# Attention with projected keys, then a gated layer: the first block's output as seven products, and three kinds of preparation moved into or out of the list-scheduled part

## The chip, the cores and the metric

The kernel runs on one core of a Trainium2 chip. The time is that of the device in microseconds, from the start of the program to its end; 517.52 us is the median of three runs of the kernel before (517.07 to 517.91). A profile is one execution taken by the hardware profiler; its span is 515.9 us.

A core has engines that each work through their own queue of instructions in order: TensorE (PE, matmuls, and PEld for loading their weights), VectorE (DVE), ScalarE (ACT), GpSimd (POOL) and SyncE (SP, which here only starts transfers). They wait for each other through semaphores. Matmuls write to eight banks of PSUM, called pF0 to pF3 and pA0 to pA3 in the kernel, each 128 partitions by 512 float32 values.

## The reference

```python
# attention: q, k, v are (8, 8, 1024, 64); E, F are (64, 1024)
k_proj = np.einsum('ks,bhsd->bhkd', E, k)
v_proj = np.einsum('ks,bhsd->bhkd', F, v)
scores = (1 / np.sqrt(64)) * np.matmul(q, k_proj.transpose(0, 1, 3, 2))
attn = softmax(scores)                  # over the 64 projected keys
attn_out = np.matmul(attn, v_proj)
# x is attn_out as (8192 tokens, 512)
# gated layer: w_gate, w_val are (512, 1536), w_out is (1536, 512)
gate = 1 / (1 + np.exp(-(x @ w_gate)))
out  = (gate * (x @ w_val)) @ w_out
```

## The kernel before

The 8192 tokens are 16 blocks of 512, two to a batch. The hidden layer of a block, `gate * val`, is kept as `hT` (1536 features on twelve tiles, 512 tokens). The output of a block is the product of that with `w_out` (`wO`).

Nearly every product of the gated layer is done as two-by-two blocks with seven products instead of eight (Winograd's form of Strassen's method). For the output the factors are sums of quarters of `hT` (`S1`, `S2`, and two made in place) and of `wO` (`T1` to `T4`). The sums are made by VectorE:

```python
def t_sums(n):        # 128 x 1536 each
    o, a, b, op, r, w = {
        3: (T3, B22, B12, ALU.subtract, ...), 2: (T2, T3, B11, ALU.add, ...),
        4: (T4, B21, T2, ALU.subtract, ...),  1: (B12, B12, B11, ALU.subtract, ...),
    }[n]
    dve(lambda e: e.tensor_tensor(o, a, b, op), r, w, t=0.95)

def s_sums(blk, n, ms, eng="DVE"):   # ms: which of six tile rows
    o, a, b, op, r, w = {
        1: (S1, A21, A22, ALU.add, "A21 A22", "S1"),
        2: (S2, S1, A11, ALU.subtract, "S1 A11", "S2"),
        3: (A21, A11, A21, ALU.subtract, "A11 A21", "A21"),
        4: (A12, A12, S2, ALU.subtract, "A12 S2", "A12"),
    }[n]
    ...
```

`product` is one of the seven: 12 matmuls of 128x256. Partial results that two quarters of the output share are copied out of a bank and into another one in between: `seed` copies bank a to bank c with ScalarE, `keep_snap` copies a bank to a half of `EF`, and `add_snap` adds a bank and such a half with VectorE.

The program has two parts. In the first, instructions stand in the order in which the code issues them: blocks 0 and 1 of the hidden layer, and the attention of batches 0 and 1. Block 0 is computed by plain products (`mstep`), and its output too:

```python
def oproj(blk, tt, pb, cols=((0, DM),)):       # 128 tokens, 12 matmuls of 128x512
    for m in range(NF):
        mm(pb, bank[pb][:, 0 : c1 - c0], hT[blk % 2][:, m, tt * P : (tt + 1) * P],
           wO[:, m, c0:c1], ..., start=(m == 0), stop=(m == NF - 1))
    dve(lambda e: e.tensor_scalar(o[:, c0:c1], bank[pb][...], 0.5, None, op0=ALU.mult), ...)
    FF.append(pb)
    add("SP", lambda e: e.dma_start(out_v[...], o[:, c0:c1]), ...)
```

The value half of block 1 is done as a chain of seven products on two banks a and c, in three steps (K = 3, 4, 5). `FF` is the list of free F banks:

```python
def p1():
    held_v["a"], held_v["c"] = a, c = FF.two()
    v_product(blk, q, a, "A11", "B11", start=True)
    seed(a, c)
def p26():
    v_product(blk, q, c, "A12", "B21", stop=True)
    v_product(blk, q, a, "S2", "T2")
    v_snap(0, a)
    hidden(K, 0, 0, bank[c][:, :], [], b=c)
# ... p57, p4
def p3():
    v_product(blk, q, c, "S4", "B22", stop=True)
    v_add(0, c)                       # VectorE, frees bank c
    FF.append(c)
    hidden(K, 1, 0, vsnap[0][:, :], [("vsnap", 0)])
```

The attention of batch 1 lies between these, in pieces that take banks from two lists, `FF` and `AA`:

```python
def mixed3():
    f, a0, a1 = FF.two(), AA.two(), AA.two()
    sc_one(3, f)                      # scores of head pair 3
    xo_one(0, a0); xo_one(1, a1)      # attention outputs of pairs 0 and 1
    for g in range(2):
        exp_half(3, g, f); FF.append(f[g])
    later("A0", x_half, 0, a0, AA)    # ScalarE copies to xu, which free the banks
    later("A1", x_half, 1, a1, AA)
def outputs3():
    f, a0 = FF.two(), AA.two()
    bd = AA.take()
    den8(bd)                          # sums of the exponentials
    xo_one(2, f); xo_one(3, a0)
    ...                               # copies to xu, reciprocals, split
def bc(rnd):                          # broadcast the reciprocals, then four multiplies into xT
    bks = [AA.take() for _ in range(4)]
    ...
```

In the code's order, `todo` is a list of slots and `put` and `on` hang further pieces after a slot:

```python
for m in range(2, NF):
    todo.append(lambda m=m: mstep(0, m))
# ...
on(3, 0, h_sums(1, Z, 1, 2, 3))
for tt in range(4):
    todo.append(lambda tt=tt: oproj(0, tt, FF.take()))
on(3, 1, n1["outputs"])
on(3, 2, lambda: n1["bc"](0))
on(3, 3, lambda: n1["bc"](1))
```

The second part is recorded as tasks with a goal and an assumed length, and a list scheduler (`arranged`) puts them in order on each engine. It covers the output of block 1, the other 14 blocks and the attention of the batches from 2 on:

```python
for n in (3, 2):
    t_sums(n)
for n in (3, 2, 4):
    gt_sums(n)                        # weight sums of w_gate, 128 x 1536
gt_sums(1)
for n in (1, 2, 3, 4):
    xs_sums(2, n)
next_kv(2, -2.0)                      # projection of keys and values of batch 2
transpose_q(["kpB"])
t_sums(4)
t_sums(1)
o_chain(1, OA, OC, 0.0, 2.0, sums=False)
```

Of the kernel before, what the change touches and what calls it, by code (L numbers as in the profile page):

```python
# [237 lines left out]
def bass_linformer_attn__then__ffn_glu_sigmoid_kernel(  # L238
# [18 lines left out]
    with contextlib.ExitStack() as es:  # L257
# [30 lines left out]
        identf = within([P, P], FP32)  # L288
        bsel8f = within([P, 4, 2, 64], FP32)
        early[0], used[0] = wT[:, :, :, :].rearrange("p a b c -> p (a b c)"), 0  # L290
        bsel8 = within([P, 4, 2, 64], BF16)
        kp = within([P, NR, DH], BF16)
        rhi = within([P, 256], BF16)
        rhl = within([P, 256], BF16)
        early[0], used[0] = gT[:, :, :, :].rearrange("p a b c -> p (a b c)"), 0
        rden = within([P, 256], FP32)
        rows = within([P, 4, 32], FP32)
        ident = within([P, P], BF16)
# [173 lines left out]
        def start_loads():  # L472
            for src, rows, n in ((E, slice(0, 64), "E"), (F, slice(64, 128), "F")):
                add(
                    "SP",
                    lambda e, src=src, rows=rows: e.dma_start(EF[rows, :], src[:, :]),
                    w=[("EF", n)],
                    dma="in" + n,
                )
            for i in range(4):  # L480
                pool(
                    lambda e, i=i: e.memset(quad[32 * i : 32 * i + 32, :], 32.0 * i),  # L482
                    w=[("quad", i)],
                )
            for R in range(2):
                load_kv_heads(0, k, R)
                load_q_half(0, 0, R)
            for R in range(2):
                load_kv_heads(1, v, R)
            load_w(0, 0)  # L490
            load_w(0, 1)
            load_w(1)
            load_w(2)
            for R in range(2):
                load_q_half(0, 1, R)
            load_w(3)
            load_w(4)
            load_w(5)

        def heads8():  # L500
# [454 lines left out]
        def attention(b):  # L955
# [87 lines left out]
                    [("rhl", R) for R in range(2)],  # L1043
                )

            def bc(rnd):
                bks = [AA.take() for _ in range(4)]
                for half_ in range(2):
                    for j in range(4):
                        jj = slice(32 * j, 32 * j + 32)  # L1050
                        mm(
                            bks[j],
                            bank[bks[j]][:, 256 * half_ : 256 * half_ + 256],
                            bsel8[jj, 2 * half_ + rnd, :, :].rearrange("p h d -> p (h d)"),
                            rhl[jj, 0:256],
                            ["bsel8", ("rhl", j // 2)],
                            tp=(32 * j, 0),
                        )
                for j in range(4):
                    n = 4 * rnd + j  # L1060
                    mul(n // 2, n % 2, bks[j])
                    AA.append(bks[j])

            def xo_one(r, bks):
                for g in range(2):
# [216 lines left out]
        def mm_one(blk, m, i, n, pb):  # L1282
# [8 lines left out]
                stop=(i == NI - 1),  # L1291
            )

        def gate(blk, m, pg, pv):
            M = blk * NF + m
# [17 lines left out]

        def oproj(blk, tt, pb, cols=((0, DM),)):
            o = vsnap[tt][:, :] if tt < 2 else ost[:, tt, :]
            ok = [("vsnap", tt)] if tt < 2 else None
            t = 2 * (2 * (blk % 2) + tt % 2) + tt // 2
            for n, (c0, c1) in enumerate(cols):
                if n:
                    pb = FF.take()  # L1320
                for m in range(NF):
                    mm(
                        pb,
                        bank[pb][:, 0 : c1 - c0],
                        hT[blk % 2][:, m, tt * P : (tt + 1) * P],
                        wO[:, m, c0:c1],
                        [("hT", blk % 2, m, tt // 2)] + (["wO0", "wO12"] if m < H6 else ["wO1"]),
                        start=(m == 0),
                        stop=(m == NF - 1),
                    )  # L1330
                dve(
                    lambda e, pb=pb, c0=c0, c1=c1: e.tensor_scalar(
                        o[:, c0:c1], bank[pb][:, 0 : c1 - c0], 0.5, None, op0=ALU.mult
                    ),
                    [],
                    ok or [("ost", tt, x) for x in ((0, 1) if len(cols) == 1 else (n,))],
                    b=pb,
                )
                FF.append(pb)
                add(  # L1340
                    "SP",
                    lambda e, c0=c0, c1=c1: e.dma_start(out_v[blk // 2, t][:, c0:c1], o[:, c0:c1]),
                    r=ok or [("ost", tt, x) for x in ((0, 1) if len(cols) == 1 else (n,))],
                    dma=f"out{tt}" if n == 0 else "outlast",
                )

        H6 = NF // 2

        def t_sums(n):
            B11, B12 = wO[:, 0:H6, 0:256], wO[:, 0:H6, 256:512]
            B21, B22 = wO[:, H6:NF, 0:256], wO[:, H6:NF, 256:512]
            T4, T3, T2 = [wT[:, i, :, :] for i in range(3)]
            o, a, b, op, r, w = {
                3: (T3, B22, B12, ALU.subtract, ["wO1", "wO12"], [("wT", 3)]),
                2: (T2, T3, B11, ALU.add, ["wO0", ("wT", 3)], [("wT", 2)]),
                4: (T4, B21, T2, ALU.subtract, ["wO1", ("wT", 2)], [("wT", 4)]),  # L1360
                1: (B12, B12, B11, ALU.subtract, ["wO0"], ["wO12", ("wT", 1)]),
            }[n]
            if n == 4:
                w = w + ["bsel8", ("kp", 0), ("kp", 1)]
                w += [(k, R) for k in ("rhi", "rhl") for R in range(2)]
            dve(lambda e: e.tensor_tensor(o, a, b, op), r, w, t=0.95)

        def s_sums(blk, n, ms, eng="DVE"):
# [4 lines left out]
            S1, S2 = hS[:, 0, lo, :], hS[:, 1, lo, :]  # L1373
# [13 lines left out]

        def part(blk, x, up):
            if x[0] == "S":
                return [(x, m) for m in up]  # L1390
            return [("hT", blk % 2, m + H6 * (x[2] == "2"), int(x[1]) - 1) for m in up]

        def product(blk, bk, A, B, start=False, stop=False, js=(0, 1), ms=(0, NF // 2), also=()):
            h = hT[blk % 2]
            for j in js:
                for m in range(*ms):
                    if A[0] == "S":
                        lhsT = hS[:, int(A[1]) - 1, m, j * P : (j + 1) * P]
# [64 lines left out]
        def evac(bk, tok, col):  # L1463
            o, keys = quarter(tok, col)
            act(o, bank[bk][:, :].rearrange("p (j c) -> p j c", j=2), [], keys, b=bk, scale=0.5)

        def o_chain(blk, a, c, goal, step, sums=True):
            turn = [0]
# [123 lines left out]
        def gt_sums(n, part=None):  # L1592
# [15 lines left out]
            if n != 1:  # L1608
                w += ["rows", "ident"] + [("rden", c, R) for c in range(2) for R in range(2)]
# [327 lines left out]

        A, Z = (0, 4), (4, 6)
        todo.append(lambda: first_pair(0, lambda: xo(1)))
        for m in range(2, NF):  # L1940
            todo.append(lambda m=m: mstep(0, m))
        qt2, sc2, den2, bc2, xo2 = half_unit(1, att)
        put(3, lambda: (qt2(0, ("DVE", "ACT")), qt2(1, ("DVE", "ACT"))))
        put(4, lambda: (sc2(0), sc2(1)))
        put(4, second_loads)
        put(6, lambda: (den2(), xo2(0), xo2(1)))
        put(7, lambda: (vt_sums(3, 0), vt_sums(2, 0)))
        put(8, lambda: bc2(0)())
        put(9, lambda: bc2(1)())
        put(10, x_sums(1, 1, 2))  # L1950
# [51 lines left out]
                on(u, 0, lambda: [late1(x, g) for x in ("A0", "A1") for g in range(2)])  # L2002
        on(2, 0, h_sums(1, A, 1))
        on(2, 4, h_sums(1, A, 2, 3))
        on(3, 0, h_sums(1, Z, 1, 2, 3))
        for tt in range(4):
            todo.append(lambda tt=tt: oproj(0, tt, FF.take()))
        on(3, 1, n1["outputs"])
        on(3, 2, lambda: n1["bc"](0))
        on(3, 3, lambda: n1["bc"](1))  # L2010

        for i, slot in enumerate(todo):
            slot()
# [9 lines left out]
        def when(K):  # L2023
            return PACE * (K - 6)

        blocks_ready(1)
        blocks_ready(2)

# [4 lines left out]
            vd_one(XA, 0, b % 2)  # L2033
            vd_one(XA, 1, b % 2, b > 3)

        for n in (3, 2):
            t_sums(n)
        for n in (3, 2, 4):
            gt_sums(n)
        gt_sums(1)  # L2040
        for n in (1, 2, 3, 4):
            xs_sums(2, n)
        next_kv(2, -2.0)
        transpose_q(["kpB"])
        t_sums(4)
        t_sums(1)
        o_chain(1, OA, OC, 0.0, 2.0, sums=False)
        for n in (1, 2, 3, 4):
            xs_sums(3, n)
# [78 lines left out]
```

The softmax here doesn't subtract the row's maximum and nothing guards it: scores larger than these inputs give would overflow.

## Time and profile before

| | |
|---|---|
| time, median of 3 (us) | 517.52 |
| span of the profile (us) | 515.9 |
| VectorE busy in 60-70, 70-80, 80-90 us (of 10 each) | 8.0, 8.8, 9.5 |
| ScalarE busy in the same (of 10 each) | 8.0, 5.5, 4.4 |
| one 128x512 VectorE operation from PSUM (us) | 0.69 |
| one 128x512 ScalarE copy from PSUM (us) | 0.60 |
| sum of weights, 128x1536 bf16, VectorE (us) | 0.95 |

The profile names an instruction by the line of the helper that recorded it, so all matmuls have line 385, and one tells them apart by the tensors they read and the bank they write. The start of one matmul to the start of the next is what it costs; its own busy time (0.27 us for 256 columns) overlaps the following ones. VectorE's and ScalarE's operations too start about 0.1 us before the one ahead has ended by the profile.

### The profile page before, as it was taken

How to read it: one execution, taken by the hardware profiler on the slowest of the kernel's cores; microseconds unless marked ns; L12 is line 12 of the kernel's file. 1: busy time of each engine (PE TensorE's matmuls, PEld its weight loads, DVE VectorE, ACT ScalarE, POOL GpSimd, SP SyncE). 2: the span in 40 equal slices, each digit the busy share in tenths (PEclk: the TensorE clock that was granted, in tenths of full speed). 3: DMA queues.
4: the chain of work that ended last, by engine and by line, in shares of the span. 5: the costliest groups of instructions: out<-in, count | busy, mean ns of one | idle time of the engine just before them, and what ended most of it. 6: DMA issues, size and time to landing. Idle time of an engine off the chain costs nothing.

```text
span 515.9 us, 11369 instructions
## 1 busy us (share of the span) xinstructions
PE 505.0 (98%) x4598; PEld 410.0 (79%) x4598; DVE 410.9 (80%) x809; ACT 345.0 (67%) x645; POOL 41.0 (8%) x60
## 2 busy tenths in 40 slices
PE   5999999999999999999999999999999999999996
PEld 3545645888888888888888888888888888888885
DVE  4548779899789796988879888797969898777774
ACT  2555683867778677677767776777676766676652
POOL 9420301200200020000100020000000000000000
PEclk9999999999999999999999999999999999999999
DMA  9999999899798788454946389374104330201013
GB/s 161 199 198 204 150 195 221 115 178 233 93 224 155 152 150 138 102 125 123 174 85 154 60 152 203 56 164 100 46 7 97 42 104 1 83 1 76 6 43 124
DMA packets 105205, 63.13 MB, mean 122 GB/s; under 512 B 63040, under 2 KB 97344, under 8 KB 105152
## 3 DMA queue, kind: packets, MB, share of 16 engines
q0 software_dynamic: 34000, 29.89, 37.5%
q1 hardware_dynamic: 71152, 32.52, 28.8%
q8 instruction: 36, 0.59, 0.4%
q14 instruction: 17, 0.14, 0.1%
HBM read 60.29 MB, written 16.78 MB: 149 GB/s over the span
## 4 chain that ended last, share of the span: by engine, by line
PE 94%; DMA 2%; DVE 1%; POOL 1%; issue 0%; ACT 0%; DVEq 0%; POOLq 0%
PE pA L385 51%; PE pF L385 43%; DMA KVs<-in_v_dram 2%; DVE hT L1832 0%; POOL KVs L403 0%; DVE vsnap L1710 0%; POOL Qb L403 0%; DVE xT L868 0%; DVE ost L1437 0%; ACT sig L389 0%; DVE sig L1786 0%; ACT vsnap L389 0%; DVE ost L1522 0%; POOL quad L482 0%; DVE hS L1382 0%
## 5 line engine op out<-in xcount | busy, mean ns | idle before, releaser
L389 ACT ACTIVATE sig<-pA 128x512 f32<-128x512 f32 x126 | 75.1, 596 | 43.4 <-PE pA L385 42.8
L1699 ACT ACTIVATE pF<-pA 128x512 f32<-128x512 f32 x99 | 58.5, 591 | 30.9 <-PE pA L385 26.3
L1710 DVE TENSOR_TENSOR vsnap<-pF,vsnap 128x512 f32<-128x512 f32 x90 | 61.8, 686 | 18.1 <-ACT vsnap L389 9.2
L1786 DVE TENSOR_TENSOR sig<-pF,sig 128x512 f32<-128x512 f32 x84 | 57.5, 685 | 7.2 <-PE pA L385 3.7
L385 PE MATMUL pF<-wO,hT 128*128 128x256 bf16 (+1 forms) x402 | 59.3, 285 | 0.0
L389 ACT ACTIVATE vsnap<-pA 128x512 f32<-128x512 f32 x84 | 50.2, 597 | 11.9 <-PE pA L385 11.8
L1832 DVE SCALAR_TENSOR_TENSOR hT<-sig,vsnap 128x512 bf16<-128x512 f32 x84 | 56.6, 683 | 0.9
L389 ACT ACTIVATE sig<-sig 128x512 f32<-128x512 f32 x84 | 52.8, 629 | 2.9 <-DVE sig L1786 2.6
L385 PE MATMUL pF<-xS,wV 128*128 128x256 bf16 x360 | 54.0, 273 | 0.1
L385 PE MATMUL pA<-xT,gT 128*128 128x256 bf16 x336 | 50.4, 273 | 0.0
L385 PE MATMUL pF<-xS,wG 128*128 128x256 bf16 x336 | 50.4, 273 | 0.0
L385 PE MATMUL pA<-xT,vT 128*128 128x256 bf16 x336 | 50.4, 273 | 0.0
L385 PE MATMUL pF<-xT,wG 128*128 128x256 bf16 (+1 forms) x264 | 50.2, 311 | 0.2 <-DVE xT L868 0.2
L389 ACT ACTIVATE sig<-pF 128x512 f32<-128x512 f32 x66 | 39.5, 598 | 15.0 <-PE pF L385 13.1
L385 PE MATMUL pA<-wT,hT 128*128 128x256 bf16 x360 | 48.8, 273 | 0.1
L1832 DVE SCALAR_TENSOR_TENSOR hT<-sig,pF 128x512 bf16<-128x512 f32 x42 | 28.7, 683 | 24.6 <-PE pF L385 24.4
L385 PEld LDWEIGHTS pF<-wO,hT 128*128 128x128 bf16 x402 | 38.7, 98 | 10.5 <-issue 0.8
L385 PE MATMUL pF<-xT,wV 128*128 128x256 bf16 (+1 forms) x240 | 41.5, 294 | 0.0
L385 PEld LDWEIGHTS pF<-xS,wV 128*128 128x128 bf16 x360 | 34.9, 98 | 6.1 <-DVE vsnap L1710 0.4
L385 PEld LDWEIGHTS pA<-wT,hT 128*128 128x128 bf16 x360 | 34.3, 98 | 5.6 <-ACT EF L389 0.8
L389 ACT ACTIVATE eT<-pA 128x512 bf16<-128x512 f32 x58 | 34.1, 596 | 5.7 <-PE pA L385 4.4
L385 PEld LDWEIGHTS pA<-xT,vT 128*128 128x128 bf16 x336 | 32.3, 98 | 5.2 <-issue 0.4
(159 smaller groups left out, 906.5 us busy)
## 6 DMA issues: line engine op xcount, KB each, us to landing
out_dram<-ost SPq DMA_DIRECT2D x61, 256.0 KB, 2.5
Qb<-in_q_dram POOLq DMA_DIRECT2D x7, 1024.0 KB, 11.9
KVs<-in_k_dram POOLq DMA_DIRECT2D x7, 1024.0 KB, 13.7
KVs<-in_v_dram POOLq DMA_DIRECT2D x7, 1024.0 KB, 18.0
wO<-in_moe_w_out_dram POOLq DMA_DIRECT2D x2, 768.0 KB, 9.8
wG<-in_moe_w_gate_dram POOLq DMA_DIRECT2D x5, 256.0 KB, 18.9
wV<-in_moe_w_val_dram POOLq DMA_DIRECT2D x5, 256.0 KB, 19.4
KVs<-in_k_dram POOLq DMA_DIRECT2D x2, 512.0 KB, 9.3
```

The costliest lines, as they stand in the source:

```text
L385: return add("PE", lambda e: e.matmul(o, lhsT, rhs, **kw), r=r, x=[("bank", b)])
L389: return add("ACT", lambda e: e.activation(o, i, func, scale=scale), r=r, w=w, x=x, t=t)
L1699: lambda e: e.activation(bank[c][:, :], bank[a][:, :], AF.Copy, scale=1.0),
L1710: lambda e: e.tensor_tensor(o, bank[bk][:, :], o, ALU.add),
L1786: dve(lambda e: e.tensor_tensor(o, bank[bk][:, :], o, ALU.add), [key], [key], b=bk)
L1832: lambda e: e.scalar_tensor_tensor(o, sg.rearrange("p (j c) -> p j c", j=2), 1.0, x.rearrange("p (j c) -> p j c", j=2), ALU.add, ALU.mult,),
```

## The change

The output of block 0 is no longer four plain products with 12 matmuls of 512 columns each, but seven products of 12 matmuls of 256 columns, done in pieces (`o_pieces`) in the order A11*B11, A12*B21, S1*T1, S2*T2, A21*T3, A22*T4, A12*B22. For that the sums that it needs are made earlier: `S1` and `S2` of block 0 lie in `EF` and in `xS[0]`, which are free then. To have pairs of quarters early, the tiles of block 0's hidden layer are computed in the order 0, 1, 6, 7, 2, 3, 8, 9, 4, 5, 10, 11, and the weights are loaded in that order. The sums of `wO` (`t_sums`) move from the list-scheduled part to the first part. Those of `w_gate` (`gt_sums`) are cut in three parts, the first of which is also made in the first part.

In exchange, three things move to the list-scheduled part: the second spread of the reciprocals (`bc(1)`), the partial weight sums (parts 1 and 2), and the last sums of block 1 (`s_sums(1, n, Z)`). Small tables (`bsel8`, `rhi`, `rhl`) get memory of their own, so that `gT` and `wT` can be written earlier.

The diff, cut to its core:

```diff
             load_w(0, 0)
             load_w(0, 1)
+            load_w(3)
             load_w(1)
-            load_w(2)
             for R in range(2):
                 load_q_half(0, 1, R)
-            load_w(3)
             load_w(4)
+            load_w(2)
             load_w(5)
...
-            def bc(rnd):
-                bks = [AA.take() for _ in range(4)]
+            def bc(rnd, goal=None, bks=None):
+                if goal is None:
+                    bks = [AA.take() for _ in range(4)]
+                    bc_mm(rnd, bks)
+                else:
+                    with group(goal, 0.5):
+                        bc_mm(rnd, bks)
...
+        def o_pieces(blk):
+            a, c = FF.two()
...
+            return [
+                do(p(a, "A11", "B11", True), lambda: seed(a, c)),
+                do(p(c, "A12", "B21"), lambda: evac(c, 0, 0)),
+                do(p(a, "S2", "T2"), lambda: keep_snap(0, a)),
+                p(c, "S1", "T1", True),
+                do(p(a, "A21", "T3"), lambda: keep_snap(1, a), lambda: add_snap(1, c, 1, 1)),
+                do(p(a, "A22", "T4"), lambda: evac(a, 1, 0), lambda: stored(blk, (2, 3))),
+                do(p(c, "A12", "B22"), lambda: add_snap(0, c, 0, 1), lambda: stored(blk, (0, 1))),
+                lambda: (FF.append(a), FF.append(c)),
+            ]
...
-        for m in range(2, NF):
+        for m in (6, 7, 2, 3, 8, 9, 4, 5, 10, 11):
             todo.append(lambda m=m: mstep(0, m))
...
-        on(3, 0, h_sums(1, Z, 1, 2, 3))
-        for tt in range(4):
-            todo.append(lambda tt=tt: oproj(0, tt, FF.take()))
+        o0 = []
+        on(2, 8, lambda: (o0.extend(o_pieces(0)), o0[0]()))
+        todo.extend([lambda n=n: o0[n]() for n in (1, 3, 2, 4, 5, 6, 7)])
+        on(3, 0, lambda: [t_sums(n) for n in (3, 1, 2)])
         on(3, 1, n1["outputs"])
-        on(3, 2, lambda: n1["bc"](0))
-        on(3, 3, lambda: n1["bc"](1))
+        on(3, 1, lambda: t_sums(4))
+        on(3, 3, h_sums(0, (0, 6), 4))
+        on(3, 4, lambda: n1["bc"](0))
+        for n in (3, 2):
+            put(5, lambda n=n: gt_sums(n, 0))
+        put(5, lambda: gt_sums(4, 0))
+        put(3, h_sums(0, (0, 2), 1, 2))
+        put(4, h_sums(0, (0, 2), 3))
+        on(1, 8, h_sums(0, (2, 6), 1, 2, 3))
+        on(1, 1, lambda: gt_sums(1, 0))
...
+        n1["bc"](1, 0.5, (GA, OA, VA, XB))
         blocks_ready(1)
         blocks_ready(2)
...
-        for n in (3, 2):
-            t_sums(n)
-        for n in (3, 2, 4):
-            gt_sums(n)
-        gt_sums(1)
+        for n in (1, 2, 3):
+            s_sums(1, n, Z)
+        for part_ in (1, 2):
+            for n in (3, 2, 4, 1):
+                gt_sums(n, part_)
         for n in (1, 2, 3, 4):
             xs_sums(2, n)
-        next_kv(2, -2.0)
+        next_kv(2, 3.0)
         transpose_q(["kpB"])
-        t_sums(4)
-        t_sums(1)
         o_chain(1, OA, OC, 0.0, 2.0, sums=False)
```

More of the change, by code (lines that the diff above doesn't have):

```diff
@@ L290, in bass_linformer_attn__then__ffn_glu_sigmoid_kernel @@
         early[0], used[0] = wT[:, :, :, :].rearrange("p a b c -> p (a b c)"), 0
-        bsel8 = within([P, 4, 2, 64], BF16)
         kp = within([P, NR, DH], BF16)
-        rhi = within([P, 256], BF16)
-        rhl = within([P, 256], BF16)
-        early[0], used[0] = gT[:, :, :, :].rearrange("p a b c -> p (a b c)"), 0
+        bsel8 = sbuf("bsel8", [P, 4, 2, 64], BF16)
+        rhi = sbuf("rhi", [P, 256], BF16)
+        rhl = sbuf("rhl", [P, 256], BF16)
         rden = within([P, 256], FP32)
@@ L1044, in split, with bc_mm @@
                 )
-            def bc(rnd):
-                bks = [AA.take() for _ in range(4)]
+            def bc(rnd, goal=None, bks=None):
[5 more added lines that the diff above has]
+                        bc_mm(rnd, bks)
+                for j in range(4):
+                    n = 4 * rnd + j
+                    mul(n // 2, n % 2, bks[j])
+                    AA.append(bks[j])
+            def bc_mm(rnd, bks):
                 for half_ in range(2):
@@ L1058, in bc @@
                         )
[L1059 to L1062, printed above, removed]
             def xo_one(r, bks):
@@ L1292, in mm_one @@
             )
+        turns = [0]
         def gate(blk, m, pg, pv):
-            M = blk * NF + m
+            M = turns[0]
+            turns[0] += 1
             sg = sig[M % 3]
@@ L1312, in gate @@
             )
[L1314 to L1345, printed above, removed]
         H6 = NF // 2
@@ L1359, in t_sums @@
                 2: (T2, T3, B11, ALU.add, ["wO0", ("wT", 3)], [("wT", 2)]),
-                4: (T4, B21, T2, ALU.subtract, ["wO1", ("wT", 2)], [("wT", 4)]),
+                4: (T4, B21, T2, ALU.subtract, ["wO1", ("wT", 2), ("rhl", 0)], [("wT", 4)]),
                 1: (B12, B12, B11, ALU.subtract, ["wO0"], ["wO12", ("wT", 1)]),
@@ L1363, in t_sums, with S_of @@
             if n == 4:
-                w = w + ["bsel8", ("kp", 0), ("kp", 1)]
-                w += [(k, R) for k in ("rhi", "rhl") for R in range(2)]
+                w = w + [("kp", 0), ("kp", 1), "rows", "ident"]
+                w += [("rden", c, R) for c in range(2) for R in range(2)]
             dve(lambda e: e.tensor_tensor(o, a, b, op), r, w, t=0.95)
+        def S_of(blk):
+            if blk:
+                return [hS[:, x, :, :] for x in range(2)]
+            return [
+                EF[:, 0:768].bitcast(BF16).rearrange("p (m c) -> p m c", c=256),
+                xS[0][:, :, :, :].rearrange("p a i c -> p (a i) c"),
+            ]
         def s_sums(blk, n, ms, eng="DVE"):
@@ L1372, in s_sums @@
             A12, A22 = h[:, hi, 0:256], h[:, hi, 256:512]
-            S1, S2 = hS[:, 0, lo, :], hS[:, 1, lo, :]
+            S1, S2 = (x[:, lo, :] for x in S_of(blk))
             o, a, b, op, r, w = {
@@ L1389, in part @@
             if x[0] == "S":
+                if blk == 0:
+                    return [
+                        [("EF", "E"), ("EF", "F"), ("snap", 0), ("snap", 1)],
+                        [("xS", 0, k) for k in (1, 2, 4)],
+                    ][int(x[1]) - 1] + [(x + "z", m) for m in up]
                 return [(x, m) for m in up]
@@ L1397, in product @@
                     if A[0] == "S":
-                        lhsT = hS[:, int(A[1]) - 1, m, j * P : (j + 1) * P]
+                        lhsT = S_of(blk)[int(A[1]) - 1][:, m, j * P : (j + 1) * P]
                     else:
@@ L1465, in evac, with p, do @@
             act(o, bank[bk][:, :].rearrange("p (j c) -> p j c", j=2), [], keys, b=bk, scale=0.5)
+        def o_pieces(blk):
+            a, c = FF.two()
+            def p(*x):
+                return lambda: product(blk, *x)
+            def do(*fns):
+                return lambda: [fn() for fn in fns]
+            return [
+                do(p(a, "A11", "B11", True), lambda: seed(a, c)),
[6 more added lines that the diff above has]
+                lambda: (FF.append(a), FF.append(c)),
+            ]
         def o_chain(blk, a, c, goal, step, sums=True):
@@ L1607, in gt_sums @@
             w = [("gT", n, j) for j in js]
-            if n != 1:
-                w += ["rows", "ident"] + [("rden", c, R) for c in range(2) for R in range(2)]
             if n == 1:
@@ L1946, in bass_linformer_attn__then__ffn_glu_sigmoid_kernel @@
         put(6, lambda: (den2(), xo2(0), xo2(1)))
-        put(7, lambda: (vt_sums(3, 0), vt_sums(2, 0)))
+        put(6, lambda: (vt_sums(3, 0), vt_sums(2, 0)))
         put(8, lambda: bc2(0)())
```

## The prediction

> **What bounds the kernel now.** I read four views of the profile of before: the page's shares and slices, the chain of work that ended last, TensorE's own timeline from 38 to 130 us, and all engines' timelines around 62 to 86 us, where the change lands. First the page (shares of each engine, the granted clock by slice, the chain by engine):
>
> ```profile
> PE 505.0 (98%) x4598; PEld 410.0 (79%) x4598; DVE 410.9 (80%) x809; ACT 345.0 (67%) x645; POOL 41.0 (8%) x60
> PEclk9999999999999999999999999999999999999999
> PE 94%; DMA 2%; DVE 1%; POOL 1%; issue 0%; ACT 0%; DVEq 0%; POOLq 0%
> ```
>
> TensorE is the chain, at full clock. A busy share proves little, so I took the spacing of starts. In the steady part a group of four 256-column matmuls follows the last every 0.437 us, 0.1093 us each; 512-column ones in the first part come every 0.216 us. With these spacings I looked from 38 to 130 us for starts later than the work before explains. There is hardly any: 0.27 us at 69.02, about 0.45 us between 85.35 and 93.23 (68 matmuls x 0.1093 = 7.43 us in 7.88), else only 0.1 us at changes of the array's tiling. So nothing can be won here but matmul columns and about 0.7 us of waits; every new wait of TensorE costs its full length. These are the block that the change replaces, TensorE's timeline (start, length, count):
>
> ```profile
> 70.08 0.74 PE L385 MATMUL pA<-eT,vpD 64*64 64x512 bf16 x8
> 70.74 2.76 PE L385 MATMUL pF<-wO,hT 128*128 128x512 bf16 x12
> 73.44 0.62 PE L385 MATMUL pA<-eT,dsel 128*32 128x256 bf16 x16
> ...
> 74.55 2.76 PE L385 MATMUL pF<-wO,hT 128*128 128x512 bf16 x12
> ...
> 77.57 2.76 PE L385 MATMUL pF<-wO,hT 128*128 128x512 bf16 x12
> ...
> 80.80 2.76 PE L385 MATMUL pF<-wO,hT 128*128 128x512 bf16 x12
> ```
>
> Four groups of twelve, each 2.70 us to the next start, fill the time between the small attention pieces. Under them ScalarE's and VectorE's work for the attention of batch 1 runs unseen. Second, how close the block-1 chain sits (all engines, 62 to 66 us):
>
> ```profile
> 63.07 0.69 DVE L1710 TENSOR_TENSOR vsnap<-pF,vsnap 128x512 f32<-128x512 f32 x1
> ...
> 64.44 0.60 ACT L1699 ACTIVATE pF<-pF 128x512 f32<-128x512 f32 x1
> ...
> 65.09 0.33 PEld L385 LDWEIGHTS pF<-xT,wV 128*128 128x128 bf16 x4 [0.38 <-ACT pF L1699]
> 65.10 0.61 PE L385 MATMUL pF<-xT,wV 128*128 128x256 bf16 x4
> ```
>
> VectorE's last read of bank F2 (63.07) frees it, ScalarE seeds it (64.44 to 65.03), and TensorE's A12*B21 starts 0.07 us later, just as the gate matmuls before it end (65.04). There is no slack on ScalarE's side here, and 0.7 us on VectorE's.
>
> **What the Trainium skill says.** "TensorE: Matmul & The Clock Gate", section Back-to-back issue gap, gives 262 cycles for 256 columns and 518 for 512 at 2.4 GHz; the trace's 0.1093 and 0.216 us are just that, so 256-column products lose about 1% against 512-column ones. "PSUM — Partial Sum Buffer", section Engine vs sequencer instructions: ScalarE and VectorE queues are strict FIFO, and matmuls start in program order. The trace agrees (65.09 above waits though later work is ready), and it is why an operation placed early in a queue delays what stands behind it. The same page, section PSUM bank collisions, has accesses of a bank by two engines kept apart; the kernel does so by bank: a product that adds to a bank waits for the copy out of it.
>
> **The change part by part.** The plain output of block 0 is 4 x 2.70 = 10.80 us of TensorE. Seven products are 7 x 12 = 84 matmuls of 256 columns, 84 x 0.1093 = 9.18 us. Saved: 1.62 us. The rest of TensorE's work is the same, part moved; from about a quarter of the program on, the order on TensorE (the last 823 of 1077 merged rows) is identical, so the outcome is settled before about 135 us.
>
> VectorE loses four copies (4 x 0.6) and gets the S sums (3.5 us in all) and the two added copies; the weight sums (four of 0.87 for wO, four of 0.87 for wG) are moved and cut. I followed the new order queue by queue with the durations of before. In the first 60 us the additions fall into VectorE's waits (2.26 us at 34.4, 2.48 us at 57.8) and cost TensorE nothing; the new order of loads has the same size at each place. Then:
>
> 1. Three S sums of 128x1024 stand ahead of the add at 63.07. Such a sum takes 0.60 to the next start, 0.72 where it is needed at once (50.33 to 51.05): 1.92 us. The add moves to 64.97, its end to 65.66, the seed to 65.72-66.30, A12*B21 from 65.10 to 66.36. TensorE: +1.26.
> 2. The new chain holds two of the four F banks from its first product. The scores of pair 3 now take the bank of block 1's last product and wait for its add: drain 0.16, add 0.69, hand-offs 0.09, less the 0.1 of the tiling change: +0.85.
> 3. A11*B11 now runs ahead of these scores, so only A12*B21 (1.31 us) is left between the attention outputs and the sums of exponentials; before it was 2.70. Those sums need a bank that the third of four xu copies frees. ScalarE ran two exponentials and four copies back to back (70.34 to 73.39); with the same work behind the later scores the third copy ends 0.8 after TensorE is ready: +0.8.
> 4. S2*T2, A21*T3 and A22*T4 add to one bank, with a copy out between. A round trip is 0.16 of drain, 0.08 to start, 0.58 copy, 0.06 back, some 0.85. Between the first two there is nothing else: +0.82. Between the second two stand the eight small broadcasts: +0.4.
> 5. The second broadcast group needs a bank whose multiply (the fourth of a queue of 0.61 each, after the added copy) ends late: +0.4.
>
> Sum of new waits 1.26 + 0.85 + 0.8 + 0.82 + 0.4 + 0.4 = 4.53 us. Removed: the 0.27 at 69.02 (A11*B11 fills it), and most of the 0.45 after 85.35, since the scheduled part now starts with half the weight sums already made. Net -1.62 + 4.53 - 0.27 - 0.45 = +2.19 us: 517.5 + 2.2 = 519.7 us.
>
> **Rivals.** (a) Only the columns count: the author's purpose, 1.6 saved plus the 0.7 of waits removed, 515.2. For it speaks that TensorE is the bound and that VectorE is freed at 84 to 97 us, where it ran weight sums without pause. Against it, that nearly nothing waited there, so relief has 0.45 us to give, and that the seven products form one chain on two banks with little between.
> (b) VectorE becomes the bound: it has 8.8 and 9.5 us of 10 busy in 70-80 and 80-90, and at the end of the chain queues added copies and eight multiplies behind each other until about 88.8. If TensorE's first products of the scheduled part then wait for multiplies or sums, another 1 to 2 us come on top: 521 to 522. By my queue the multiplies end 0.4 before they are needed.
> (c) The transfers: wO's halves land 8.4 to 11.3 us after issue at 58.4 and 59.3, so at 66.8 to 70.6, and the new chain wants the first at about 70. Before, it wanted it at 70.7. If the late one is the first, up to 0.3 us; the second is wanted 2 us after it lands. Hidden, I think. The key transposes for batch 2 start some 4 us later but have about 4 us before the first head.
>
> **Range and chances.** The sizes of waits 2 to 5 depend on each other: a delay at one lets ScalarE or VectorE catch up before the next. If half of them vanish, 518; if only wait 1 stays, about 516.5; with (b), 522. Range 516.8 to 521.8. Two per cent is 10 us, more than the whole block costs: faster 0.01, same 0.98, slower 0.01.
>
> **What would show it.** TensorE's timeline of after: A12*B21 of block 1's last third at 66.4 instead of 65.1, its weight load released by the ScalarE seed, and three VectorE sums of 128x1024 before the add; scores of pair 3 released by that add; idle before the sums of exponentials, released by an xu copy; waits before A21*T3 and A22*T4 on the EF copies; batch 2's projection ending at about 88 instead of 85.35. If that projection ends at 84 or earlier, the waits are wrong and (a) holds; if it ends as said and the tail is late by more than 3 us, it is (b). I would be wrong most likely by waits that overlap, making the loss smaller.

## The result, and the profile after

| | before | after |
|---|---|---|
| time, median of 6 (us) | 517.47 (516.99 to 518.38) | 525.30 (522.4 to 527.09) |
| ratio to before, 95% interval | | 1.015 (1.0119 to 1.0181) |
| span of the profiled execution (us) | 515.9 | 523.3 |

The change loses 7.8 us. 519.7 was predicted, with a range up to 521.8, so some 5.6 us came from something that the prediction did not have. The page of after (shares of each engine, granted clock in 40 slices, the chain by engine):

```profile
span 523.3 us, 11457 instructions
...
PE 505.2 (97%) x4634; PEld 414.0 (79%) x4634; DVE 414.2 (79%) x822; ACT 348.9 (67%) x650; POOL 41.0 (8%) x60
...
PEclk9999999999989999999999999999999999999999
...
PE 89%; DMA 5%; ACT 2%; DVE 2%; POOL 1%; issue 1%; DVEq 0%; ACTq 0%; POOLq 0%
```

TensorE has the same busy time as before, 505 us. Two things are new: the chain has 5% of DMA in place of 2%, and one slice of the clock, the twelfth (144 to 157 us), reads 8. Neither lies where the change lies. First the place where it does, TensorE's timeline of after (start, length, count, idle time before and who ended it):

```profile
66.14 0.61 PE L384 MATMUL pF<-xT,wV 128*128 128x256 bf16 x4 [1.12 <-ACT pF L1702]
...
70.06 1.47 PE L384 MATMUL pF<-wO,hT 128*128 128x256 bf16 x12
71.37 0.60 PE L384 MATMUL pF<-xS,wV 128*128 128x256 bf16 x4
71.90 0.40 PE L384 MATMUL pF<-qT,kpD 64*64 64x512 bf16 x1
72.76 0.41 PE L384 MATMUL pF<-qT,kpD 64*64 64x512 bf16 x3 [0.45 <-DVE vsnap L1713]
...
75.84 0.62 PE L384 MATMUL pA<-eT,dsel 128*32 128x256 bf16 x16 [0.82 <-ACT xu L388]
...
80.43 1.48 PE L384 MATMUL pF<-wT,hT 128*128 128x256 bf16 x12 [0.69 <-ACT EF L388]
...
82.69 1.47 PE L384 MATMUL pF<-wT,hT 128*128 128x256 bf16 x12 [0.45 <-ACT EF L388]
84.00 1.47 PE L384 MATMUL pF<-wO,hT 128*128 128x256 bf16 x12
85.40 0.59 PE L384 MATMUL pA<-rhl,bsel 32*128 32x256 bf16 x3
...
86.03 1.92 PE L384 MATMUL pA<-KVs,EFT 128*64 128x512 bf16 x16
87.88 0.61 PE L384 MATMUL pA<-xT,wG 128*128 128x256 bf16 x4
```

This is the seam, and the five waits that show a releaser were foretold, with these releasers; the one foretold ahead of the second broadcast (85.40) shows none. A product of twelve costs 1.31 us (70.06 to 71.37), and the projection of batch 2 ends at 87.88 (foretold 88). So far after is some 2 us behind. The rest is lost 60 us later, in a part whose order on TensorE is the same in both kernels. The list of waits of TensorE in after has an entry that before has not:

```profile
PE pA L384 <- DMA xu<-kpd: 3.7, 1, 3.7
```

`xu<-kpd` is the transposing transfer (a DMA that transposes on its way) that writes the transposed keys `kpB` (in `xu`'s memory) for the next batch. The timeline of all engines of before around it, transfers and first head only (SPq and POOL rows are issues of transfers):

```profile
131.50 1.29 SPq L937 DMA_TRANSPOSE xu<-kpd  x1
...
137.75 0.88 POOL L403 DMA_DIRECT2D KVs<-in_k_dram  x1 [36.88 <-PE pA L385]
...
143.35 0.38 PE L385 MATMUL pA<-qT,xu 128*128 128x512 bf16 x1
```

and the same of after:

```profile
137.54 0.88 POOL L402 DMA_DIRECT2D KVs<-in_v_dram  x1 [33.32 <-PE pF L384]
138.07 1.29 SPq L936 DMA_TRANSPOSE xu<-kpd  x1
...
149.29 0.61 PE L384 MATMUL pA<-qT,xu 128*128 128x512 bf16 x1 [3.68 <-DMA xu<-kpd]
```

Before issues the keys' transfer at 131.50, with the loads of batch 4 (the keys' first, the values' right behind at 138.62) only after it has landed, and the head of batch 3 comes 11.9 us later. After issues it at 138.07, half a microsecond behind the 1 MB load of the values of batch 4, and TensorE wants the head at 145.45, 7.4 us later. The keys' transfer of before in the list of transfers between 120 and 152 us (time from issue to landing):

```profile
xu<-kpd SPq DMA_TRANSPOSE x1, 5.0
```

and the two transfers of after in the same list (KB each where it is given):

```profile
KVs<-in_v_dram POOLq DMA_DIRECT2D x1, 1024.0 KB, 11.3
...
xu<-kpd SPq DMA_TRANSPOSE x1, 11.2
```

The six transfers of this kind in after take 3.1 at best and 3.2 us in the median, this one 11.2; in before they take 3.1 to 5.0. And after the wait the clock is gone. Stretches of after (length, busy time of PE, PEld, DVE, ACT, POOL with counts, granted clock, DMA share, GB/s):

```profile
149.00:150.00 1.00, 0.71 (x3) 0.38 (x4) 0.00 (x0) 0.06 (x1) 0.00 (x0) 0.50 0.46 164
150.00:151.00 1.00, 1.00 (x7) 0.69 (x6) 0.00 (x0) 1.00 (x2) 0.96 (x2) 0.50 0.06 25
...
152.00:153.00 1.00, 1.00 (x11) 0.83 (x9) 0.30 (x1) 0.60 (x1) 0.00 (x0) 0.85 0.71 83
```

In stretches of 0.1 us, the half clock reaches from 148.9 to 152.3. From start to start, the wait is 3.84 us longer than the work before it explains, and the groups from 149.29 to 152.50 take 1.5 us more than the same four in before (143.35 to 145.09). With the seam, 2.1 + 3.8 + 1.5 = 7.4 us, by which the two spans differ.

### The profile page after: what moved, and what is told of

It reads as the page before. It is cut to its first block, busy times and chain, and to the rows that moved or that the text cites. A ratio compares the mean times of both kernels' runs of the same rounds, so it can differ in the third digit from the quotient of the medians.

```text
span 523.3 us, 11457 instructions
## 1 busy us (share of the span) xinstructions
PE 505.2 (97%) x4634; PEld 414.0 (79%) x4634; DVE 414.2 (79%) x822; ACT 348.9 (67%) x650; POOL 41.0 (8%) x60
## 4 chain that ended last, share of the span: by engine, by line
PE 89%; DMA 5%; ACT 2%; DVE 2%; POOL 1%; issue 1%; DVEq 0%; ACTq 0%; POOLq 0%
PE pA L384 49%; PE pF L384 41%; DMA KVs<-in_v_dram 2%; DMA xu<-kpd 2%; DVE vsnap L1713 1%; ACT xu L388 1%; DVE hT L1835 0%; ACT EF L388 0%; POOL KVs L402 0%; POOL Qb L402 0%; ACT kpd L388 0%; ACT sig L388 0%; ACT vsnap L388 0%; ACT eT L388 0%; ACT pF L1702 0%
## 5 line engine op out<-in xcount | busy, mean ns | idle before, releaser
L384 PE MATMUL pF<-wO,hT 128*128 128x256 bf16 x390 | 53.4, 275 | 0.0
L388 ACT ACTIVATE sig<-pF 128x512 f32<-128x512 f32 x66 | 39.5, 598 | 15.0 <-PE pF L384 11.3
## 6 DMA issues: line engine op xcount, KB each, us to landing
Qb<-in_q_dram POOLq DMA_DIRECT2D x7, 1024.0 KB, 11.2
```

Of the source, the lines that this page charges most:

```text
L384: return add("PE", lambda e: e.matmul(o, lhsT, rhs, **kw), r=r, x=[("bank", b)])
L388: return add("ACT", lambda e: e.activation(o, i, func, scale=scale), r=r, w=w, x=x, t=t)
```

## The experiments

Theory A: the load of the values ran beside the transposing transfer and slowed it. Theory B: the transfer was late because it was issued late, behind three transposes of the queries. A third reading, tested later, is that the seam's lateness made transfers meet. Because the start of the program varies by up to 1.4 us from run to run, I give two measures: the median time, and from each profile the distance between starts of projections: from the first (at about 52 us) to batch 2's, which holds the seam alone (but not the 0.45 us that before loses right after it), and to the last (352.76 us in before).

| kernel | median (us) | ratio to before (95%) | first to batch 2's (us) | first to last (us) |
|---|---|---|---|---|
| before | 517.47 to 517.91 | | 31.26 | 300.52 |
| after | 525.30 | 1.0119 to 1.0181 | 33.98 | 308.12 |
| held load | 520.11 | 1.0032 to 1.0060 | 33.98 | 303.47 |
| before, values early | 519.61 | 1.0024 to 1.0054 | 31.26 | 301.78 |
| half the load | 520.97 | 1.0052 to 1.0088 | 33.98 | 305.08 |
| third projection earlier | 520.03 | 1.0028 to 1.0057 | 33.98 | 302.80 |
| seam's steps, load not held | 522.01 | 1.0051 to 1.0106 | 31.21 | 306.22 |
| held + earlier sums | 518.82 | 1.0011 to 1.0031 | 32.75 | 301.65 |
| held + denominators' bank | 519.97 | 1.0024 to 1.0050 | 33.93 | 302.76 |
| held + other buffers | 519.18 | 1.0017 to 1.0038 | 33.11 | 301.93 |
| held + first product earlier | 519.45 | 1.0017 to 1.0039 | 33.60 | 302.43 |
| held + all four | 517.11 | 0.9980 to 0.9993 | 31.21 | 300.03 |

**The load held back.** From the changed kernel:

```diff
-                load_v(b, done)
+                load_v(b, done + (["kpB"] if b == 4 else []))
```

> The changed kernel with one wait added: the 1 MB load of the values of batch 4 starts only when the transposed keys of batch 3 have landed; the order of instructions on every engine stays. Theory A (the transposing transfer of the keys was slowed from 3 to 11 us by that load running beside it): it lands within 5 us of its issue at about 138, the first head of batch 3 starts at about 145.5 without a wait, no matmuls run at a lower clock after it, and the time is 519.3 to 520.2 us, the kernel before plus the 2.1 us of the seam. Theory B (the transfer is late because it is issued late and stands behind the three transposes of the queries): it still lands at about 149, the head waits over 3 us, 525 us.

Measured: 520.11 us. The load is issued at 143.64 and the keys' transfer, issued at 139.21, is back at its usual time; TensorE no longer waits for it. The transfers of this run between 120 and 152 us:

```profile
KVs<-in_v_dram POOLq DMA_DIRECT2D x1, 1024.0 KB, 11.8
...
xu<-kpd SPq DMA_TRANSPOSE x1, 3.2
```

Nothing else in the order was touched, and the three transposes of the queries still stand right ahead of it (135.07 to 139.1), so theory B falls. This one wait is worth 5.2 us by the medians, 5.6 if each is counted from the kernel before in its own series, and what is left, 520.11 - 517.91 = 2.2 us, is close to the 2.19 predicted for the seam. The distance to the last projection is 2.95 us longer than in before, but 0.66 of that is lost at a wait for ScalarE at 130.88, ahead of the held load, that after does not have.

**The opposite, in the kernel before.**

```diff
-                load_v(b, done)
+                load_v(b, [] if b == 4 else done)
```

> The kernel before with one wait taken away: the load of the values of batch 4 no longer waits for the transposes of the queries of its round and the stores, so it starts at about 127, soon after the third projection, and runs beside the transposing transfer of the keys issued at 131.5. Theory A: that transfer takes 8 us or more to land instead of 3.5, but the first head of batch 3 starts at 143.4, 12 us after the issue, so the time moves by less than 0.5 us from 517.5. Theory B: the transfer still takes 3 to 5 us; the time is the same. If it lands later than 143.4, the same wait as in the changed kernel appears and costs that plus a stretch of lower clock.

Measured: 519.61, so 1.7 us slower, against at most 0.5 expected; the named transfer took 5.5 us, not 8. The load, issued at 128.46, hit another one instead. Issues on the queue of transposes, its transfers between 126 and 146 us, then VectorE and TensorE:

```profile
129.37 1.23 SPq L1221 DMA_TRANSPOSE xT<-xu  x1
130.69 5.58 SPq L885 DMA_TRANSPOSE qT<-Qb  x1
136.37 3.48 SPq L937 DMA_TRANSPOSE xu<-kpd  x1
```

```profile
KVs<-in_v_dram POOLq DMA_DIRECT2D x1, 1024.0 KB, 11.1
...
xT<-xu SPq DMA_TRANSPOSE x1, 10.8
```

```profile
140.29 0.42 DVE L1643 TENSOR_TENSOR xS<-xT 128x512 bf16<-128x512 bf16 x1 [2.44 <-DMA xT<-xu]
...
141.98 0.61 PE L385 MATMUL pA<-xT,wV 128*128 128x256 bf16 x4 [0.73 <-DVE hT L1832]
```

The transpose of the attention's output, 3.3 us in before, took 10.8; the issue of the next ones took 5.58 and 3.48 us in place of 1.29, so the keys' came 4.9 us later (4.3 counted from the first projection). VectorE waited 2.44 us for the first, and its late operations then held up TensorE by 0.73 us (0.89 from start to start) and once more by 0.3; from first to last projection the loss is 1.26 us. The theory's mechanism holds for whichever transposing transfer is under way; my guess of the victim, and with it of the cost, was wrong.

**Half the load.** From the changed kernel, the load of batch 4's values cut by heads, the second half tied to the keys:

```diff
+            if b == 4:
+                for R in range(2):
+                    hh = slice(4 * R, 4 * R + 4)
+                    load(KV[n][:, hh, :], v[b]...[:, hh, :], [("KV", n, R)], f"KV{n}{R}",
+                         r=list(after) + (["kpB"] if R else []))
+                return
```

> The changed kernel with the load of the values of batch 4 cut in two of 512 KB: the first starts where the 1 MB load started, just ahead of the transposing transfer of the keys, the second when that transfer has landed. Theory A (the transposing transfer goes slowly for as long as a load runs beside it): with half the bytes beside it, it lands in 6 to 8 us in place of 11.2, the head of batch 3 waits 0 to 1 us, no stretch of lower clock follows (0.72 came after 3.8 us of wait), and the time is 519.8 to 521.5 us. Rival (any load queued just ahead holds it back, whatever its size): the landing stays at 10 us or more and the time near 525. Rival for the clock: if matmuls slow down after the head without a wait of some us before it, the lower clock is not the wait's consequence.

Measured: 520.97 us. Transfers of this run, 128 to 155 us; TensorE's timeline; and the stretch around the head as above:

```profile
KVs<-in_v_dram POOLq DMA_DIRECT2D x2, 512.0 KB, 7.5
xu<-kpd SPq DMA_TRANSPOSE x1, 8.7
```

```profile
147.64 0.39 PE L384 MATMUL pA<-qT,xu 128*128 128x512 bf16 x1 [1.25 <-DMA xu<-kpd]
```

```profile
147.00:149.00 2.00, 1.36 (x12) 1.13 (x13) 0.28 (x1) 0.93 (x2) 0.99 (x2) 1.00 0.43 162
```

Nothing beside it 3.2 us, 512 KB 8.7, 1 MB 11.2: it grows with the load, but not in proportion; the first half costs 5.5 us, the second 2.5. It lands just after the load each time: at 147.6 us here, where the first half lands at 146.9, and at 149.2 in after, where the load lands at 148.8. I expected 6 to 8 us. The wait is 1.25 us, and the clock stays at 1.00.

**The third projection earlier.** In after the third projection starts at 131.36, in before at 125.24; the seam accounts for 2.5 us of that, the rest is the list scheduler's order. It counts 26 us for a load; with 20 for those of batch 3 it puts the third projection ten groups of matmuls earlier. From the changed kernel, with the load not held:

```diff
-            add("POOL", lambda e: e.dma_start(o, i), r=r, w=w, dma=sem, t=26.0, tie=tie)
+            add("POOL", lambda e: e.dma_start(o, i), r=r, w=w, dma=sem, t=t, tie=tie)
...   # in load_k and load_v
+                t=20.0 if b == 3 else 26.0,
```

> The changed kernel without the held load; only the time that the list scheduler assumes for the load of the keys and values of batch 3 is set to 20 us instead of 26, which puts the third kv projection about ten groups of matmuls (5 us) earlier in TensorE's order. Theory A: the transposed keys are then issued before the load of the values of batch 4 begins, land in 3 to 5 us, and the head of batch 3 doesn't wait: 519.3 to 520.5 us, as with the held load. Rival (the shift of the third projection has nothing to do with it): the transfer still takes 8 us or more and the time stays near 525.

Measured: 520.03 us. The projection starts at 126.34 instead of 131.36, the keys' transfer is issued at 130.09, 6.6 us ahead of the load, and lands after 3.3 us. The load now runs beside the last transpose of the queries, which takes 11.0 us, but TensorE does not wait for that one. So the loss needs the late place of the third projection as well as the early load, and an edit that touches no wait cures it too. Why the scheduler chose that place in after was not tried; that the goal of batch 2's projection went from -2.0 to 3.0 is the likely reason.

**All steps at the seam, load not held.** The four edits that follow, without the first:

> The four steps at the seam (earlier S sums, the other bank for the denominators, the other buffers for the partial results, the first product earlier) without the held load. Theory A (the loss at 145 us comes from the order in which load and transposing transfer are issued, which the list fixes): the whole list part moves up by 2.8 us, the loss stays, and the time is 517.1 + 5.2 = 522.3 us, 521 to 523.5. Rival (the loss came from the seam's being late, so that transfers met): without the lateness it is gone, 517 to 518 us.

Measured: 522.01 us. The seam is 2.8 us shorter, as in the version with the load held (31.21), and the collision is there, 2.7 us earlier: transfer 10.7 us, wait 3.19 us. The reading by lateness falls. The head and two stretches of this run:

```profile
146.15 0.61 PE L384 MATMUL pA<-qT,xu 128*128 128x512 bf16 x1 [3.19 <-DMA xu<-kpd]
```

```profile
151.00:152.00 1.00, 1.00 (x7) 0.71 (x5) 0.85 (x4) 0.22 (x1) 0.00 (x0) 0.51 1.25 201
152.00:153.00 1.00, 1.00 (x11) 0.90 (x10) 0.31 (x1) 0.00 (x0) 0.00 (x0) 1.00 1.21 189
```

Half clock until 152, six microseconds after the head's start at 146.15; in after it was three. In stretches of 0.1 us it begins at 145.2 and lasts 6.8 us, twice the 3.4 of after, and the collision costs 306.22 - 300.03 = 6.2 us in this profile, against the version with the load held.

The next four take the held load and one of the seam's waits each. **Earlier sums** (wait 1 of the prediction):

```diff
-        on(1, 8, h_sums(0, (2, 6), 1, 2, 3))
+        on(1, 3, h_sums(0, (2, 6), 1, 2, 3))
```

> The kernel of the held load, with the three S sums of 128x1024 put earlier among VectorE's work, at the place where it stood idle at about 58 us. If they are what delays the sum v_add, A12*B21 starts about 1.2 us sooner, with no wait for the seed on ScalarE, and the time falls by 1.1 to 1.3 us from the held load's. Rival: VectorE has no room there, something else on it is pushed back, and the time falls by less than 0.5 us or not at all.

Measured: 518.82, 1.29 us less; 33.98 - 32.75 = 1.23 us at the seam. The wait for the seed is gone from the list of waits.

**Another bank for the denominators** (wait 3):

```diff
-                f, a0 = FF.two(), AA.two()
-                bd = AA.take()
+                bd, f, a0 = FF.take(), [FF.take(), AA.take()], AA.two()
...   # and the banks go back to the lists they came from
```

> The kernel of the held load, with the denominators of batch 1 in a bank of the other ring, so that they no longer take the bank that the third copy of the attention output has to empty. If the wait of 0.82 us ahead of the denominators lies on the path, the time falls by 0.7 to 1.0 us from the held load's. Rival: the wait only moves to the next user of the bank that was given up, and the time stays within 0.3 us.

Measured: 519.97 and 33.93, no gain. The 0.82 us for the `xu` copy is gone from the list of waits, and this is in its place:

```profile
PE pF L384 <- DVE wT L1003: 0.7, 1, 0.7
```

The reciprocals (line 1003, 1.76 us) now hold a bank of the ring that S1*T1 takes next. The rival held: the wait moved to the next user.

**Other buffers for the partial results** (wait 4), with S2*T2 ahead of S1*T1:

```diff
-                do(p(a, "S2", "T2"), lambda: keep_snap(0, a)),
+                do(p(a, "S2", "T2"), lambda: keep_snap(0, a, True)),   # to vsnap
...   # A21*T3 and both add_snap likewise
-        todo.extend([lambda n=n: o0[n]() for n in (1, 3, 2, 4, 5, 6, 7)])
-        on(3, 0, lambda: [t_sums(n) for n in (3, 1, 2)])
+        todo.extend([lambda n=n: o0[n]() for n in (1, 2, 3, 4, 5, 6, 7)])
+        on(3, 0, lambda: [t_sums(n) for n in (3, 2, 1)])
```

> The kernel of the held load, with the two partial results of block 0 kept in the buffer pair that only the v stage uses otherwise, instead of in halves of the buffer EF that the accumulating products themselves read from ScalarE's copies, and with S2*T2 ahead of S1*T1. If the waits of 0.69 and 0.45 us for ScalarE's copy ahead of A21*T3 and A22*T4 lie on the path, the time falls by 0.8 to 1.0 us from the held load's 520.1, to about 519.2. Rival: the time of TensorE is only taken up by the next wait, ahead of the kv projection, and the time stays within 0.3 us.

Measured: 519.18, 0.93 less; 0.87 at the seam. The wait of 0.69 us ahead of A21*T3 is gone. This edit changes both the buffers and the order; it was not tried which of the two does it, and the order, which puts a product between the two that add to one bank, suffices as a reason.

**The first product earlier** (wait 2):

```diff
+        o0 = []
+        on(3, 0, lambda: (o0.extend(o_pieces(0)), o0[0]()))   # before mixed
...
-        o0 = []
-        on(2, 8, lambda: (o0.extend(o_pieces(0)), o0[0]()))
```

> The kernel of the held load, with the first of the seven products of block 0 emitted ahead of the scores of the third pair, so that TensorE has 12 matmuls (1.31 us) to do while VectorE finishes v_add. If the 0.45 us wait ahead of the rest of these scores lies on the path, the time falls by 0.3 to 0.6 us from the held load's 520.1. Rival: the later scores push back ScalarE's exponentials and with them the denominators, whose wait grows by the same amount; no change within 0.3 us, or slower.

Measured: 519.45, 0.66 less, with 0.38 at the seam; the wait for the denominators grew only from 0.82 to 0.90.

**All of them.**

> All five steps at once: the held load, the earlier S sums, the other bank for the denominators, the other buffers for the partial results, the first product earlier. If the seam's waits are separate and all on the path, they add: 520.1 - 1.3 - 0.9 - 0.9 - 0.4 = 516.6 us, that is 1 us under the kernel before, since what is left of the change is the 1.62 us of columns saved less the waits that it has not lost. Rival: the sums of the gaps hide one behind another, and the time stays at 518 or above, so that the change has no form that pays.

Measured: 517.11 us (21 runs), with 516.6 expected, against 517.79 of before in the same series: ratio 0.9987, 0.9980 to 0.9993, a version faster than before by 0.13%. At the seam 33.98 - 31.21 = 2.77 us come back: 1.23 + 0.87 + 0.38 from the single edits are 2.48, and 0.3 come together with the denominators' bank, which alone gave nothing: here VectorE has fewer sums ahead of the reciprocals (they start at 74.30, 75.69 with the bank alone), and S1*T1 no longer follows them at once. What is left at the seam, TensorE's timeline:

```profile
77.66 1.48 PE L384 MATMUL pF<-wT,hT 128*128 128x256 bf16 x12 [0.30 <-ACT vsnap L388]
...
79.92 1.47 PE L384 MATMUL pF<-wT,hT 128*128 128x256 bf16 x12 [0.45 <-ACT vsnap L388]
```

Two hand-overs of a bank that is added to, 0.75 us. Of the 1.62 us foretold for the columns, 0.5 (first to last projection) to 0.7 (medians) reach the end.

## Why the prediction was wrong

The steps at the seam were right, some sizes were not. The saving is there, but the sum that gave 1.62 us compared unlike things: each of the four 2.70 us holds some 0.1 us for the change of the array's tiling after it, and 84 x 0.1093 holds none. Of the products of after, those ahead of such a change take 1.40 us to the next start (84.00 to 85.40) in place of 1.31; with three such changes the saving is an estimated 1.3 us. Wait 1: A12*B21 at 66.14, 66.36 foretold; taking it away gave 1.23 us (1.26 foretold). Wait 2: foretold 0.85; from 71.90 to 72.76 are 0.86 us, but the one matmul at 71.90 needs 0.2 of them itself, and 0.45 are shown as waiting; the edit that avoids it gave 0.38. This term was too large. Wait 3: foretold 0.8, 0.99 from start to start. Wait 4: 0.82 and 0.4, measured 0.86 and 0.52 from start to start, where the eight broadcasts of before take 0.33 (0.69 and 0.45 as waiting). Wait 5: foretold 0.4; the second broadcast group runs from 85.40 to 86.03, 0.1 us longer than in before (80.27 to 80.80). Sum and sign held: +2.19 foretold, 2.2 with the load held. That the sum is so near is partly luck: the saving and waits 2 and 5 were put too large, wait 3 and the second part of wait 4 too small. In the range, half of the waits would give 517.4 by the prediction's own terms, not 518. Rival (a) fell, because the waits are on the path, each by its own edit but the third; rival (b) fell too: besides wait 2, VectorE stands among TensorE's waits of after with 0.3 and 0.2 us, as in before.

Two steps failed, and they are one. "From about a quarter of the program on, the order on TensorE (...) is identical, so the outcome is settled before about 135 us" took the same order for the same waits. The loss is at 145 us, inside that part: 3.84 us of waiting for the keys' transfer and 1.5 of half clock, because the order of issue on two other queues had changed relative to each other: the values' load before the keys' transposing transfer. And rival (c) stopped at "hidden, I think", with the transfers of the seam and of batch 2 in view: for those it was right (neither wO's halves nor batch 2's keys made TensorE wait for them), but batch 3's was never followed, and its usual 3.2 us were not asked to hold when a load runs beside it. The trace of before already showed that they need not: the two transposes of the attention's output issued from 100.66 us on, while the loads of batch 3 (issued from 98.25 on) were running, took 13.2 and 13.0 us, against a median of 3.3 for their kind. The list of waits of before has no entry for the keys' transfer, so nothing pointed there; the distance from its issue to its use, 11.9 us, would have.

On the loss the Trainium skill has two passages that the runs can be held against. "DMA: Bandwidth & Descriptors", section Queues, rings and completion order, says that a DMA engine takes queues in turn, packet by packet. The trace agrees: from 141 to 147 us of after the queue of the load moved 832 packets, 0.85 MB, and the queue of the transposing transfer 779 packets, 0.20 MB, nearly one for one. With the load held, the queue of the transposes alone moved 2152 packets in 3 us (139 to 142). By these counts a packet of the load holds about 1 KB and one of the transfer about a quarter of that, so 256 KB of the one have as many packets as 1 MB of the other, and in turns both end together. With half a load, 377 and 316 packets moved from 141 to 145 us, and as the load ended, 738 of the transposing transfer's queue in the next 2 us. "TensorE: Matmul & The Clock Gate", section HAM oscillation — how this bites in real kernels, says that an idle gap over about 3.4 us puts TensorE at half rate. The traces agree in kind: 0.50 after the gap of 3.8 us in after, 1.00 after the 1.4 us with half the load. But with the seam's steps less sufficed: TensorE was idle for 3.19 us (3.35 from start to start), and the clock fell at 145.2, 2.2 us after the last matmul had ended (142.96). The single runs show how much hangs on it: of the six of after, the fastest, 522.40, has a mean clock of 1.0, the slowest, 527.09, has 0.992.

## What to carry to other kernels

When a change leaves the bound engine's order as it is in some part, compare the order of issue on the transfer queues there as well, and for each transfer the time from issue to first use against what it takes beside another load, not alone. A wait near 3 us on a bound TensorE can cost more than itself (3.84 us cost 5.3 in after, 3.35 cost 6.2 with the seam's steps), so the first thing to take away is the longest wait, not the sum of the small ones. And a wait for a bank is removed only if the next user of the bank given up comes later than its release: the denominators' bank gave nothing alone.

## What the runs showed of the hardware that I had not expected

A transposing transfer of 256 KB (128x1024 bf16) that is issued right behind a plain load lands only when the load does: 3.2 us alone, 8.7 beside 512 KB, 10.7 to 11.2 beside 1 MB, each 0.4 to 0.7 us after the load, while the load of 1 MB hardly suffers (11.3 us in after, 11.8 with the load held, other loads following it). It is the same for other transposing transfers (3.3 to 10.8), and their issues stretch as well (1.29 to 5.58 us). Plain transfers on that queue slow too: stores of 256 KB take 2.5 us in the median, but the two that before issues from 143.81 to 146, beside the loads of batch 4 and with no transposing transfer under way, took 7.6 in the median. The half clock lasted 3.4 us in one run and 6.8 in another, after gaps of like length (3.84 and 3.35 us).
